# Top-k attention and two MLPs on one core: the planner's DMA prices are changed and the order of the work is searched again

## The chip, the cores and the metric

The kernel runs on one core of a Trainium2 chip. The metric is the device time of one execution in microseconds, the median over several runs. TensorE does matrix products, VectorE and ScalarE element work and reductions, GpSimd element work, and SyncE issues all DMA transfers of this kernel, plain and transposing ones.

## What is computed

The inputs are q, k and v of 4 batches, 8 heads, 576 positions and 64 dimensions. Each row of scores keeps its 32 largest entries, and a softmax over these weighs v. The heads are joined to 2304 tokens of 512 values, and two MLPs of 512 to 2048 to 512 follow, the first with a softplus and the second with h - tanh(h) as its nonlinearity:

```python
scores = scale * np.matmul(q, k.transpose(0, 1, 3, 2))
kth = np.partition(scores, -top_k, axis=-1)[..., -top_k:-top_k + 1]
scores = np.where(scores >= kth, scores, -1000000000.0)
attn = softmax(scores)                 # top_k = 32
x = np.matmul(attn, v)                 # heads joined: 2304 x 512
x = softplus(x @ w_in) @ w_out
h = x @ w_in2
out = (h - np.tanh(h)) @ w_out2
```

## The kernel before, in words

All matrix products are done in pairs of 16-bit numbers: each operand is split into a high and a low half, and three products replace one.

**Attention.** A visit is a pair of heads of one batch and two of its four blocks of 128 queries (32 visits). `visit_load` (L1198) loads q, k and v; `visit_prep_k` and `visit_prep_q` (L1233, L1269) scale and split k and q and transpose them by DMA into kT and qT. Where k and v serve a second visit, they are parked in device memory (kd, vd) and fetched back. A visit has four tiles of 128 x 576 scores, and half of the visits have one tile more for the left-over 64 queries of each head. For each tile, `front` (L1320) makes scores on TensorE, which ScalarE copies out; `chain` (L1368) runs seven selections on VectorE (four times the 8 largest, three times replacing them); `exps` (L1383) and `turn` (L1408) form the masked exponentials, split them into hl and issue the DMA transpose into pT; `back` (L1421) multiplies pT with v on TensorE and, after the second head, transposes the result into a chunk's input.

**Weights.** The four weight matrices come in eight groups each through `weight_load`, `weight_convert` and `weight_split` (L855 to L955), with work on ScalarE, VectorE, GpSimd and TensorE for each group. `norm` (L1010) reads the tensors a second time for a scale of each batch.

**MLPs.** Chunks of 256 tokens (and two of 128 left-over tokens) go through `mlp_step` (L1624), one group of weights a step: `gemm1`, the nonlinearity (`act1`), `gemm2`. The first MLP of a chunk needs its attention tiles, the second needs the first one's scale.

**The order.** Nothing is issued while the program text above runs. A `Recorder` (L230) keeps each engine call as an operation with a price from `price` (L319). `order` (L548) starts from the order of the text with random noise on each rank (seed `SEED`, spread `SIG`), plans forwards and backwards seven times in `place` (L440), keeps the best plan, and adds the noise of every entry of `SHIFTS`: a random seed or the names of steps, a stretch of planned time in ns, a spread or an offset in ns, and the letters of the engines (P, D, A, G, S for TensorE, VectorE, ScalarE, GpSimd, SyncE). The plan that results is the order in which each engine's queue is written out by `run` (L647, the calls themselves at L658, which is why all rows of the trace name L658). `idle` (L585) puts small keep-busy matmuls into planned gaps of TensorE.

In the plan a DMA takes SyncE's time (the first number that `price` gives), and then its traffic (the second) on one queue that all transfers share; it has landed `DLAT` later:

```python
busy = max(busy, t + 800) + o.lat
end[i] = busy + DLAT            # DLAT = 1700
```

SyncE's queue is strictly in order, so an issue that waits for its source holds all issues behind it.

Of the kernel before, what the change touches and what calls it, by code (L numbers as in the profile page):

```python
# [78 lines left out]
SEED = 219  # L79
# [5 lines left out]
SIG = 15  # L85
# [35 lines left out]
MARGP = 0.0  # L121

SHIFTS = (
# [15 lines left out]
    ("S", 201532, 209532, -1000, "PDAGS"), (30793, 419293, 427293, 1000, "PDAGS"), (3088, 194840, 202840, 400, "PDAGS"),  # L139
# [7 lines left out]
    (11067, 946337, 986337, 1000, "PDAGS"), (44392, 990466, 1030466, 6000, "PDAGS"), (82429, 1039495, 1047495, 2500, "PD"),  # L147
    (2374, 229658, 237658, 1000, "PDAGS"), (99569, 810939, 830939, 400, "SA"), (72260, 653623, 673623, 1000, "PDAGS"),
# [15 lines left out]
    (30152, 681321, 689321, 1000, "PDAGS"), (37243, 797248, 817248, 200, "PDAGS"), (88929, 199096, 219096, 200, "SA"),  # L164
# [6 lines left out]
    (3405, 588701, 738701, 200, "PDAGS"), (89568, 201552, 209552, 400, "PDAGS"), (4446, 719529, 759529, 100, "PD"),  # L171
# [58 lines left out]
class Recorder:  # L230
# [88 lines left out]
    def price(self, eng, method, a, k, outs, ins):  # L319
        out = outs[0]  # L320
# [10 lines left out]
        if eng == "SP":  # L331
            size = math.prod(out.shape) * mybir.dt.size(out.dtype)
            if "transpose" in method:
                return 1350.0, size / 164.0
# [1615 lines left out]
```

## Time and profile before

| | before |
|---|---|
| median of 3 runs | 1143.07 us (1141.26 to 1143.63) |
| the profiled execution | 1143.22 us |
| its span, first to last instruction | 1141.5 us |
| TensorE busy, matmuls | 90% of the span |
| VectorE, ScalarE, GpSimd busy | 82%, 80%, 66% |
| DMA issues on SyncE | 411 plain, 304 transposing |

The rows below come from that profiled execution, and times in them count from the span's start. PE is TensorE (PEld its weight loads), DVE is VectorE, ACT is ScalarE, POOL is GpSimd, and SPq is SyncE's queue of issues. Tile names are those of the program with the numbers left out: s are the scores, h and y the accumulators of the MLPs, px the attention output, hl the split exponentials.

### The profile page before, as it was taken

Reading aid. Unit: us, or ns where it says so; the run is one execution under the profiler, and the core shown is the slowest. Engines: PE = TensorE matmul, PEld = TensorE weight load, DVE = VectorE, ACT = ScalarE, POOL = GpSimd, SP = SyncE. Lnnn points to the kernel's source line nnn. Section 1 sums busy time; section 2 is a strip of 40 time slices with the busy share of each in tenths; the row PEclk is TensorE's granted clock in tenths of the full one; section 3 lists DMA queues with packets and bytes.
Section 4 is the critical chain, followed back from the end, with each engine's and each line's share of the span. In section 5 each row is a group of like instructions: output and inputs, shape, how many; then the busy total and the mean of one; then the engine's idle time right before and its main releaser. Section 6 shows DMA issues by size and latency. Waiting matters only on the chain.

```text
span 1141.5 us, 27974 instructions
## 1 busy us (share of the span) xinstructions
PE 1027.5 (90%) x10094; PEld 795.4 (70%) x10094; DVE 931.3 (82%) x2059; ACT 913.1 (80%) x1889; POOL 757.2 (66%) x1169
## 2 busy tenths in 40 slices
PE   4577647988989899999989999999999999999998
PEld 2334336866658777876689868976787789977965
DVE  3888989989999999999989999999999999510111
ACT  6999999999888998888889888898978777732422
POOL 3445445999778777667878677788976677543433
PEclk9698767999999999999999999999999999999999
DMA  8999997557769875546877655466665443200000
GB/s 270 286 242 253 263 237 214 166 115 157 139 150 199 168 143 102 117 86 124 185 170 150 127 107 113 78 126 131 162 119 106 78 108 70 49 6 19 2 8 22
DMA packets 323131, 153.15 MB, mean 134 GB/s; under 512 B 270256, under 2 KB 314288, under 8 KB 322992
## 3 DMA queue, kind: packets, MB, share of 16 engines
q1 hardware_dynamic: 322992, 151.36, 59.4%
q8 instruction: 79, 1.29, 0.5%
q14 instruction: 60, 0.49, 0.1%
HBM read 73.01 MB, written 15.37 MB: 77 GB/s over the span
## 4 chain that ended last, share of the span: by engine, by line
PE 49%; ACT 18%; DVE 11%; POOL 7%; DMA 7%; issue 6%; SPq 2%; ACTq 0%; POOLq 0%; DVEq 0%
PE y L658 21%; PE h L658 20%; DVE x L658 5%; PE s L658 4%; DVE m L658 4%; ACT x L658 3%; ACT ssb L658 3%; PE px L658 3%; ACT wlo L658 2%; ACT xy L658 2%; SPq L658 2%; POOL hl L658 2%; ACT hl L658 2%; ACT r L658 1%; ACT whi L658 1%
## 5 line engine op out<-in xcount | busy, mean ns | idle before, releaser
L658 PEld LDWEIGHTS <-whi 128*128 128x128 f16 (+1 forms) x3994 | 372.7, 99 | 101.4 <-DVE whi L658 27.1
L658 PE MATMUL h<-xy,whi 128*128 128x256 f16 (+1 forms) x2560 | 395.0, 262 | 5.1 <-ACT r L658 4.1
L658 PE MATMUL h<-xy,wlo 128*128 128x256 f16 (+1 forms) x1280 | 324.9, 262 | 0.0
L658 DVE MAX8 m<-x 128x8 f32<-128x576 f32 x432 | 314.9, 747 | 1.0
L658 POOL TENSOR_TENSOR hl<-x,hl 128x512 f16<-128x512 f32 (+1 forms) x288 | 213.1, 757 | 80.0 <-ACT hl L658 71.3
L658 PEld LDWEIGHTS <-wlo 128*128 128x128 f16 (+1 forms) x2002 | 197.1, 99 | 33.5 <-issue 13.9
L658 DVE MATCH_REPLACE8 x<-m,x 128x576 f32<-128x576 f32 x288 | 212.9, 740 | 0.0
L658 PE MATMUL y<-g,whi 128*128 128x256 f16 (+1 forms) x1280 | 199.4, 262 | 1.1 <-POOL g L658 1.1
L658 PE MATMUL y<-whi,g 128*128 128x512 f16 x576 | 194.2, 380 | 0.6 <-POOL g L658 0.6
L658 POOL TENSOR_TENSOR g<-r,g 128x512 f16<-128x512 f32 (+1 forms) x160 | 173.5, 1085 | 14.8 <-PE y L658 8.4
L658 PE MATMUL y<-g,wlo 128*128 128x256 f16 (+1 forms) x640 | 162.5, 262 | 0.0
L658 DVE SCALAR_TENSOR_TENSOR r<-h,hinb,r 128x512 f32<-128x512 f32 (+1 forms) x80 | 55.0, 687 | 122.4 <-ACT r L658 122.1
L658 PEld LDWEIGHTS <-g 128*128 128x128 f16 x864 | 81.6, 98 | 74.7 <-POOL g L658 1.3
L658 ACT ACTIVATE x<-ssb,nb,tiny 128x576 f32<-128x576 f32 x136 | 117.5, 865 | 6.7 <-POOL nb L658 4.2
L658 DVE MAX8 m<-ssb 128x8 f32<-128x576 f32 x144 | 107.6, 747 | 16.1 <-ACT ssb L658 12.5
L658 PEld LDWEIGHTS <-pT 128*128 128x128 f16 (+1 forms) x2240 | 87.8, 102 | 35.0 <-DMA pT<-hl 15.9
L658 PE MATMUL y<-wlo,g 128*128 128x512 f16 x288 | 109.4, 380 | 0.0
L658 DVE MATCH_REPLACE8 x<-m,ssb 128x576 f32<-128x576 f32 x144 | 106.6, 740 | 0.0
L658 PE MATMUL px<-vhl,pT 128*128 128x65 f16 (+1 forms) x2240 | 95.3, 196 | 11.8 <-DMA pT<-hl 9.4
L658 PE MATMUL s<-kT,qT 128*128 128x288 f16 x512 | 87.4, 295 | 16.6 <-ACT ssb L658 7.8
L658 POOL TENSOR_SCALAR r<-r,gsb 128x512 f32<-128x512 f32 (+1 forms) x80 | 53.8, 673 | 67.9 <-ACT g L658 65.0
L658 ACT CAST hl<-x 128x576 f16<-128x576 f32 x144 | 96.6, 671 | 2.1 <-DMA pT<-hl 2.0
(134 smaller groups left out, 1665.2 us busy)
## 6 DMA issues: line engine op xcount, KB each, us to landing
whi<-in_moe_w_in_dram SPq DMA_DIRECT2D x11, 1023.0 KB, 6.9
whi<-in_moe_w_out_dram SPq DMA_DIRECT2D x7, 1023.5 KB, 6.0
vd<-vhl SPq DMA_DIRECT2D x16, 330.0 KB, 3.5
vhl<-vd SPq DMA_DIRECT2D x16, 330.0 KB, 3.8
kd<-kT SPq DMA_DIRECT2D x32, 160.0 KB, 2.8
kT<-kd SPq DMA_DIRECT2D x32, 160.0 KB, 3.0
xy<-in_moe_w_out_dram SPq DMA_DIRECT2D x18, 255.8 KB, 3.1
qraw<-in_q_dram SPq DMA_DIRECT2D x64, 64.0 KB, 2.5
```

The lines of the kernel that those rows point to most:

```text
L658: fn(*a, **k)
```

## The change

In `price`, a DMA issue on SyncE and the traffic of a transposing DMA are priced anew, by size; the constants `PTC` and `SPC` are new; `SEED` and `SIG` have other values, and `SHIFTS` has other entries throughout. The operations that are recorded are the same. The condition on 128,000 elements takes in pT (128 x 9 x 128) and qT (128 x 8 x 128); the other transposes (kT, the chunk input, the left-over queries) are below it. The list of `SHIFTS` is cut to an entry of each.

```diff
-SEED = 219
+SEED = 12130
...
-SIG = 15
+SIG = 150
...
+PTC = 1600.0
+SPC = 640.0
 
 SHIFTS = (
-    (65854, 156749, 196749, 100, "PD"), (28308, 218614, 226614, 200, "PDAGS"), (28963, 611250, 761250, 1000, "S"),
...
+    (46389, 1013650, 1033650, 6000, "P"), ("L3", 21785, 321785, -1000, "PDAGS"), (76838, 41833, 101833, 2500, "S"), (75144, 482483, 502483, 400, "A"),
...
         if eng == "SP":
             size = math.prod(out.shape) * mybir.dt.size(out.dtype)
             if "transpose" in method:
-                return 1350.0, size / 164.0
-            return 540.0, size / 330.0
+                return (PTC if math.prod(out.shape) >= 128 * 1000 else 1335.0), size / 230.0
+            kb = size // 1024
+            return (770.0 if kb == 32 else 690.0 if kb == 16 else 550.0 if kb in (230, 232) else SPC), size / 330.0
```

## Rows read from the trace of the kernel before

**Rows 1.** The head of the page: busy us, share of the span, instructions.

```profile
span 1141.5 us, 27974 instructions
PE 1027.5 (90%) x10094; PEld 795.4 (70%) x10094; DVE 931.3 (82%) x2059; ACT 913.1 (80%) x1889; POOL 757.2 (66%) x1169
```

**Rows 2.** Stretches: length, busy us of PE, PEld, DVE, ACT, POOL, clock, DMA share, GB/s.

```profile
0.00:100.00 100.00, 61.66 (x331) 34.27 (x332) 69.59 (x171) 84.65 (x169) 42.71 (x74) 0.86 0.96 271
100.00:200.00 100.00, 63.19 (x502) 43.41 (x501) 95.96 (x209) 94.71 (x192) 51.04 (x75) 0.73 0.95 234
...
250.00:300.00 50.00, 42.95 (x423) 33.07 (x422) 46.81 (x117) 44.55 (x107) 44.70 (x77) 0.97 0.67 137
300.00:350.00 50.00, 43.71 (x441) 31.65 (x439) 47.18 (x103) 45.13 (x96) 40.78 (x67) 1.00 0.70 154
350.00:400.00 50.00, 45.53 (x488) 39.37 (x485) 47.46 (x99) 45.04 (x100) 38.04 (x58) 1.00 0.86 180
...
550.00:600.00 50.00, 44.98 (x490) 39.84 (x491) 46.76 (x94) 43.01 (x90) 38.85 (x59) 1.00 0.84 177
...
1000.00:1142.00 142.00, 137.41 (x1160) 101.97 (x1158) 16.80 (x33) 47.89 (x78) 52.58 (x68) 1.00 0.04 11
```

**Rows 3.** Waits of PE, 300 to 400 us: total us, times, longest.

```profile
PE px L658 <- DMA pT<-hl: 4.6, 3, 2.5
...
PE s L658 <- DMA kT<-khl: 1.7, 1, 1.7
...
PE px L658 <- DMA ql<-in_q_dram: 0.3, 1, 0.3
```

**Rows 4.** Waits of PE, 500 to 600 us.

```profile
PE s L658 <- DMA kT<-khl: 2.2, 1, 2.2
...
PE px L658 <- DMA pT<-hl: 0.3, 1, 0.3
```

**Rows 5.** Chain of waits, 300 to 400 us: shares by line, two pieces (start, us).

```profile
by line: ACT x L658 11.2%; issue 11.2%; SPq L658 10.7%; ACT ssb L658 8.2%; ACT r L658 6.8%; PE h L658 4.3%; ACT hl L658 4.2%; DMA xy<-in_q_dram 4.0%; ACT g L658 3.7%; ACT xy L658 3.6%; DMA pT<-hl 3.2%; DMA out_dram<-r 2.9%; ACT vhl L658 2.5
...
318.10 2.77 SPq L658
320.92 2.07 DMA kraw<-in_k_dram
```

**Rows 6.** SyncE's issues in order of time: start us, us; 99 before the last.

```profile
301.40 1.23 SPq L658 DMA_TRANSPOSE qT<-qhl  x1
...
400.26 1.27 SPq L658 DMA_TRANSPOSE qT<-qhl  x1
```

**Rows 7.** DMA issues, 300 to 400 us: the transposes, count, us to landing.

```profile
pT<-hl SPq DMA_TRANSPOSE x16, 3.5
...
xy<-xs SPq DMA_TRANSPOSE x10, 3.0
kT<-khl SPq DMA_TRANSPOSE x8, 3.2
...
qT<-qhl SPq DMA_TRANSPOSE x5, 3.1
...
qlT<-zq SPq DMA_TRANSPOSE x1, 3.6
```

**Rows 8.** The tile hl on SyncE, 0 to 200 us: issue ns min/median/max, landing.

```profile
L658 SPq DMA_TRANSPOSE pT<-hl x19: 1247/1672/3048, 38.2 to 185.5; - x19
...
DMA to landing us min/median/max: 3.2/4.9/8.0
```

**Rows 9.** The same tile, 200 to 1000 us.

```profile
L658 SPq DMA_TRANSPOSE pT<-hl x125: 1241/1302/2449, 202.0 to 994.9; - x125
...
DMA to landing us min/median/max: 3.2/3.4/5.8
```

More of the change, by code (lines that the diff above doesn't have):

```diff
@@ L121 @@
 MARGP = 0.0
+PTC = 1600.0
+SPC = 640.0
 SHIFTS = (
[15 rows of a table removed]
-    ("S", 201532, 209532, -1000, "PDAGS"), (30793, 419293, 427293, 1000, "PDAGS"), (3088, 194840, 202840, 400, "PDAGS"),
[7 rows of a table removed]
-    (11067, 946337, 986337, 1000, "PDAGS"), (44392, 990466, 1030466, 6000, "PDAGS"), (82429, 1039495, 1047495, 2500, "PD"),
-    (2374, 229658, 237658, 1000, "PDAGS"), (99569, 810939, 830939, 400, "SA"), (72260, 653623, 673623, 1000, "PDAGS"),
[15 rows of a table removed]
-    (30152, 681321, 689321, 1000, "PDAGS"), (37243, 797248, 817248, 200, "PDAGS"), (88929, 199096, 219096, 200, "SA"),
[6 rows of a table removed]
@@ L171 @@
-    (3405, 588701, 738701, 200, "PDAGS"), (89568, 201552, 209552, 400, "PDAGS"), (4446, 719529, 759529, 100, "PD"),
[3 rows of a table removed]
-    (17909, 633166, 693166, 400, "PDAGS"), (74182, 365812, 373812, 2500, "PDAGS"), (56364, 400295, 420295, 400, "PDAGS"),
-    (50012, 680208, 688208, 100, "PDAGS"), (68348, 383507, 443507, 100, "PDAGS"), (76410, 778623, 786623, 400, "SA"),
-    (75530, 760685, 800685, 100, "PDAGS"), (50157, 374022, 382022, 6000, "P"), (53770, 707888, 715888, 2500, "S"),
[5 rows of a table added]
+    (19788, 400133, 420133, 400, "PDAGS"), ("S", 163120, 183120, -1000, "PDAGS"), (33840, 34058, 42058, 400, "PDAGS"),
@@ new lines @@
+    (91963, 167971, 317971, 200, "PDAGS"), (12879, 782422, 932422, 200, "SA"), (27238, 666144, 686144, 400, "PDAGS"),
[6 rows of a table added]
+    (2845, 4981, 12981, 200, "PDAGS"), ("M0", 235551, 243551, 20000, "PDAGS"), ("N3", 88964, 2000000, 1000, "PDAG"),
[14 rows of a table added]
+    (25487, 951743, 959743, 6000, "PDAGS"), ("W2", 119002, 127002, -20000, "PDAGS"), (72190, 952161, 992161, 6000, "PDAGS"),
+    (92249, 94967, 154967, 400, "A"), (85508, 225447, 245447, 400, "A"), ("", 84359, 104359, 6000, "PDAGS"), (89908, 58046, 78046, 1000, "P"),
@@ new lines @@
+    (31139, 640882, 660882, 2500, "PD"), (92698, 518700, 526700, 6000, "S"), (79721, 490224, 510224, 1000, "P"),
+    ("P,V", 145208, 153208, -3000, "PDAGS"), (24195, 952178, 972178, 6000, "PDAGS"), (5990, 993454, 1033454, 6000, "PDAGS"),
[8 rows of a table added]
+    ("N1", -1000000, 2000000, 1000, "PDAG"), (39132, 752468, 760468, 6000, "SA"), ("P,V", 18550, 26550, 20000, "PDAG"),
[5 rows of a table added]
+    (21444, 206084, 356084, 400, "S"), ("P,V", 207673, 227673, 1000, "PDAG"), (42558, 1058825, 1098825, 6000, "PDAGS"),
[7 rows of a table added]
+    (6879, 321015, 329015, 1000, "PDAGS"), (94692, 660386, 668386, 1000, "PDAGS"), (90813, 273459, 281459, 1000, "PDAGS"),
[3 rows of a table added]
@@ new lines @@
+    (76968, 457854, 477854, 200, "PDAGS"), (16248, 233733, 241733, 400, "SA"), (79456, 536193, 576193, 100, "PDAGS"),
[4 rows of a table added]
+    (16761, 658114, 678114, 1000, "PDAGS"), ("P,V", 288782, 296782, 1000, "PDAGS"), (77901, 263268, 283268, 100, "PDAGS"),
+    (66200, 283996, 291996, 2500, "G"), (78609, 444485, 452485, 2500, "PDAGS"), (23524, 311989, 461989, 200, "P"), (76392, 617559, 637559, 2500, "G"),
+    (2987, 588914, 608914, 200, "PDAGS"), (11702, 219958, 239958, 200, "PDAGS"), (37011, 586508, 606508, 6000, "P"),
@@ L178 @@
+    (51336, 618911, 678911, 200, "PDAGS"), (44460, 645705, 653705, 200, "PDAGS"), (50763, 654609, 662609, 400, "SA"),
[4 rows of a table added]
 )
```

100 rows, old and new, of the table SHIFTS are left out of this document.

## The prediction

> **What bounds the kernel now.** I read the head of the page first: which engine is busiest. TensorE leads with 1027.5 us of a span of 1141.5 us, and VectorE and ScalarE follow within ten points [rows 1]. No instruction is meant to change its work, so what a new order can move is the part of the span in which TensorE stands idle: 1141.5 - 1027.5 = 114.0 us. The table of stretches says where it lies [rows 2]. The first 100 us hold 100 - 61.66 = 38.3 us of it and the second 36.8 us; 250 to 300 us holds 7.1, 300 to 400 us holds 6.29 + 4.47 = 10.8, 550 to 600 us holds 5.0. The last 142 us are TensorE's alone (137.41 us busy, VectorE 16.80), so the end is set by TensorE, and every microsecond that it stops idling earlier ends the program a microsecond sooner, as long as the work that it would do is ready.
>
> The two idle parts have different causes. From 0 to 200 us the clock is also low: the granted clock is 0.86 and then 0.73, so TensorE ran partly at 1.2 and partly at 2.4 GHz; the DMA engines are 0.96 and 0.95 busy, and in the second 100 us VectorE and ScalarE are at 95.96 and 94.71 us [rows 2]. That opening is full on four resources at once. From 300 to 400 us nothing but VectorE is as full, yet TensorE waits. There I asked for TensorE's waits: 4.6 us for the transposed probabilities (pT), 1.7 us for transposed keys, 0.3 us behind a query load, 6.6 us together, all of them for DMAs [rows 3]. In 500 to 600 us it is 2.2 + 0.3 = 2.5 us [rows 4].
>
> The chain of waits through 300 to 400 us shows SyncE's queue with 10.7% of that stretch, beside DMA landings of 4.0, 3.2 and 2.9%; one piece of it is an issue of 2.77 us on SyncE, directly followed by the landing of a key load that had queued behind it [rows 5]. SyncE's own sequence of issues says why: the first issue after 301.40 us and the one at 400.26 us are 98.86 us apart, with 99 issues back to back [rows 6]. The list of DMA issues has the 99 by kind; 16 + 5 + 10 + 8 + 1 = 40 are transposes [rows 7], so 59 are plain. SyncE's queue is the pace there.
>
> **The change, part by part.** It alters prices in the planner and the random draws by which it orders the work, and so the order on all five engines' queues. Transfers, tiles and arithmetic stay: by instruction the sum of removed and added work is nothing. Only the small keep-busy matmuls that the planner puts into planned TensorE gaps can change in number; they stand in gaps, and I cost them at nothing. If a gap is smaller on the chip than planned, they lie on TensorE's path, and the plan's gaps differ between both kernels by no amount that a row shows.
>
> *Issue prices.* Old prices of the 99 issues: 40 x 1.35 + 59 x 0.54 = 85.9 us, against 98.86 us in the trace. New prices: pT and the transposed queries have over 128,000 elements, so 21 x 1.6 us, the other 19 x 1.335 us, and the 59 plain ones at the default of 0.64 us (some sizes have 0.55 to 0.77): 33.6 + 25.4 + 37.8 = 96.7 us. So in this stretch the old planner thought SyncE some 13 us faster than it is, the new one 2 us. What it put on TensorE for the moment in which a transpose should have landed came late on the chip; a planner that knows this puts other matmuls there or issues the transpose ahead of loads that can wait. What it can win is the wait for DMAs on TensorE, 6.6 us [rows 3] and 2.5 us [rows 4]: I take both whole, **-9.1 us**. The bounds: nothing at the upper end, because another late input can take each wait's place (ScalarE sits at 45 of 50 us in both halves of 300 to 400 us); at the lower end all of TensorE's idle time in the two stretches, 10.8 + 5.0 = 15.8 us. I take the waits since they are the row nearest to what the edit touches.
>
> *Overpriced issues.* After 200 us a pT issue takes 1.302 us in the middle of 125 [rows 9], so 1.6 us is too much there by 0.3 us less the gap between two issues; in the opening it takes 1.672 us [rows 8], and 1.6 is right. The planner will leave SyncE about a quarter of a microsecond of room per pT. I cost it at 0: TensorE has matmuls of the two MLPs queued, which need no pT. Without that cover, TensorE would be given a pT later than it could have it; the bounds are 0 and a loss of 2.5 us, the waits of the weaker stretch [rows 4], since a plan that waits needlessly can at worst undo what it won there.
>
> *Traffic prices.* A pT moves 128 x 9 x 128 x 2 = 294,912 bytes: 1.80 us of queue before at 164 bytes per ns, 1.28 us after at 230. With the 0.8 us to start and 1.7 us to land that the planner adds, an unhindered pT lands after 4.3 us by the old price and 3.8 us by the new; the trace has 3.4 us after 200 us [rows 9], so the new price is the better one for 125 of 144. In the opening it has 4.9 us [rows 8], and there the old price is nearer. The 19 pT of the opening are now 19 x 0.52 = 9.8 us cheaper in the plan, in a stretch whose DMA engines the trace shows full. I take 0 for the opening, since VectorE, ScalarE and the DMAs are all full there and an order cannot shorten them; bounds are 9.8 us to either side, the one amount by which the plan of the opening is known to move.
>
> Queues passed: since every order is drawn anew, an issue on SyncE that is moved ahead holds all behind it for 1.3 us (transpose) or about 0.6 us (plain), whoever waits for them; the 2.77 us piece above is the worst that the chain shows [rows 5].
>
> The sum: the profiled execution took 1143.22 us for its span of 1141.5, 0.15 us above the median of 1143.07. 1143.22 - 9.1 = 1134.1, on the scale of the median **1134.0 us**.
>
> A rule against this: the Trainium skill, page "DMA: Bandwidth & Descriptors", section "Issuing engines are not separate DMA queues", says that the sequencer's time to start a DMA is usually small relative to the DMA itself. By that rule issue prices would decide nothing and the sum would be 0, at 1143.1 us. This case's trace does not agree for 300 to 400 us, where 99 issues fill 98.86 us.
>
> **The rivals.** *No change, 1143.1 us.* The waits for DMAs are real but not binding: when TensorE gets pT earlier, it meets the next late thing, ScalarE's copies or VectorE's selection, which run at 47 of 50 us in 300 to 400 us. For it: VectorE is nearly full there. Against it: TensorE's own waits name DMAs for 6.6 of its 10.8 us of idle time there [rows 3]. The same result would come if the change did not do what it says because plain orders barely move; the much wider first draw (150 in place of 15) speaks against that. Chance 0.17.
>
> *Slower, 1152.9 us.* The one mechanism: the opening. The plan now has 9.8 us less DMA time for the same pT transfers, packs weight and norm loads into it, and on the chip the engines are already 0.96 busy [rows 2], so the weights' last groups and the first transposes land later by that much. It decides when that lateness is more than VectorE's and ScalarE's queued work covers; taken whole, 1143.1 + 9.8 = 1152.9 us. For it: 4.9 us to land in the opening against 3.8 planned. Against it: TensorE has so much idle time there that lateness may be absorbed. Chance 0.23.
>
> *Much faster, 1117.5 us.* The new draw also finds a better opening: 1143.1 - 15.8 - 9.8. For it: 75.1 us idle on TensorE by 200 us and 30.4 us on VectorE in the first 100. Against it: no price that governs the opening's arithmetic was touched. Chance 0.10.
>
> **How the numbers follow.** My own case, TensorE's waits for DMAs shrinking, has 0.50 and its own range is 1127 (1143.1 - 15.8) to 1141. With 0.2% (2.3 us, about what a measurement of this kernel can tell from no change), faster is 0.50 + 0.10 = 0.60, same 0.17, slower 0.23. The range that should hold 8 in 10 reaches down to 1121, leaving out the better part of the much faster case, and up to 1152, just short of the slower rival's whole price: 1121 to 1152 us, predicted 1134.0.
>
> **What would show it.** Right: TensorE's busy time stays near 1027 us and its idle time falls; waits of TensorE for pT and transposed keys in the stretch where SyncE issues back to back fall from 6.6 us to under 3; 99 issues still take about 99 us. Slower rival: idle time of TensorE up to 200 us grows beyond 75 us, with pT landing above 4.9 us there. No change: the waits for DMAs are gone, but waits for ScalarE or VectorE of the same size stand in their place. The forecast is wrong if the idle time moves mainly in stretches where neither SyncE nor the DMA engines are full: then the draws, not the prices, made the difference.

## The result, and the profile after

The changed kernel takes 1127.92 us, the median of 4 runs, against 1143.34 us for the kernel before (with a fourth run); the ratio is 0.9871, with a 95% interval from 0.9854 to 0.9888. The profiled execution took 1127.21 us, with a span of 1125.5 us. Forecast were 1134.0 us and a range from 1121 to 1152 us.

The head of the changed kernel's page, with the first line of its chain of waits:

```profile
span 1125.5 us, 27898 instructions
PE 1022.8 (91%) x10078; PEld 796.4 (71%) x10078; DVE 921.3 (82%) x2059; ACT 913.8 (81%) x1889; POOL 751.7 (67%) x1169
...
PE 51%; ACT 16%; DVE 13%; POOL 8%; issue 6%; DMA 5%; SPq 0%; POOLq 0%; ACTq 0%; DVEq 0%
```

Against [rows 1], TensorE is idle for 1125.5 - 1022.8 = 102.7 us in place of 114.0 us, and busy for 4.7 us less; together that is the 16.0 us between the two spans. VectorE, ScalarE and GpSimd have the same number of instructions. SyncE's queue has gone from the chain; in the kernel before it had 2% of it:

```profile
PE 49%; ACT 18%; DVE 11%; POOL 7%; DMA 7%; issue 6%; SPq 2%; ACTq 0%; POOLq 0%; DVEq 0%
```

The changed kernel by stretches, with the columns of [rows 2]:

```profile
0.00:100.00 100.00, 56.62 (x310) 31.75 (x311) 67.28 (x165) 83.23 (x165) 39.86 (x77) 0.85 1.00 281
100.00:200.00 100.00, 66.41 (x497) 45.60 (x497) 95.28 (x214) 94.39 (x197) 48.53 (x74) 0.74 0.90 229
...
250.00:300.00 50.00, 40.92 (x435) 32.59 (x434) 49.85 (x121) 45.50 (x108) 44.95 (x79) 0.97 0.66 142
300.00:350.00 50.00, 49.90 (x474) 37.37 (x471) 49.18 (x115) 47.00 (x101) 44.57 (x70) 1.00 0.75 156
350.00:400.00 50.00, 46.47 (x485) 39.51 (x484) 47.40 (x104) 46.19 (x100) 40.06 (x60) 0.97 0.81 178
...
550.00:600.00 50.00, 50.00 (x602) 45.56 (x600) 49.80 (x105) 46.36 (x98) 45.92 (x67) 1.00 0.84 172
...
1000.00:1126.00 126.00, 121.18 (x1003) 89.64 (x1000) 13.93 (x25) 42.48 (x68) 47.12 (x60) 1.00 0.03 12
```

The opening has not gained: up to 200 us TensorE is busy for 56.62 + 66.41 = 123.0 us, before 124.85, at much the same granted clock (0.85 and 0.74). From 300 to 400 us its idle time falls from 10.8 to 0.10 + 3.53 = 3.6 us, and in 550 to 600 us from 5.0 to none.

TensorE's waits in the changed kernel, first all of 300 to 400 us and then all of 500 to 600 us:

```profile
PE s L678 <- ACT ssb L678: 3.2, 2, 1.7
PE s L678 <- DVE n L678: 0.3, 1, 0.3
...
PE s L678 <- ACT ssb L678: 0.2, 1, 0.2
```

No wait for a DMA is left in either stretch; [rows 3] had 6.6 us and [rows 4] 2.5 us of them. SyncE is about as full as it was:

```profile
300.92 1.23 SPq L678 DMA_TRANSPOSE qT<-qhl  x1
...
399.83 0.57 SPq L678 DMA_DIRECT2D kraw<-in_k_dram  x1
```

These are the first and the last issue of the same stretch in the changed kernel, in the form of [rows 6]; 97 issues start between 300 and 400 us, where the kernel before had 99. What changed is mainly which issue stands where, not how many there are.

**The plan and the chip.** `order` gives each of SyncE's 715 issues a planned start. They keep their sequence on the chip, so planned and measured starts can be subtracted one by one; this is the mean lag of the chip behind the plan in us:

```
issues that start in   150-200  250-300  350-400  450-500  600-650  900-950
kernel before             10.3     18.4     27.6     28.7     37.2     39.9
changed kernel            12.2     17.6     21.2     21.4     21.6     24.2
```

Both orders fall behind alike up to 300 us. Then the old one loses 9.2 us between 250-300 and 350-400 us and 8.5 us between 450-500 and 600-650 us; the new one loses 3.6 and 0.2 us there. In the kernel before, these two steps enclose the stretches in which SyncE hardly pauses: from 300 to 400 us there are three pauses of more than 0.2 us between two issues, 2.2 us together, and from 542 to 596 us there is none. The old plan promised transposes earlier than SyncE could start them.

### The profile page after: what moved, and what is told of

Its sections match the earlier page's. It is cut to its first block, busy times and chain, and to the rows that moved or that the text cites. A ratio compares the mean times of both kernels' runs of the same rounds, so it can differ in the third digit from the quotient of the medians.

```text
span 1125.5 us, 27898 instructions
## 1 busy us (share of the span) xinstructions
PE 1022.8 (91%) x10078; PEld 796.4 (71%) x10078; DVE 921.3 (82%) x2059; ACT 913.8 (81%) x1889; POOL 751.7 (67%) x1169
## 4 chain that ended last, share of the span: by engine, by line
PE 51%; ACT 16%; DVE 13%; POOL 8%; issue 6%; DMA 5%; SPq 0%; POOLq 0%; ACTq 0%; DVEq 0%
PE h L678 23%; PE y L678 21%; DVE x L678 5%; DVE m L678 5%; PE s L678 5%; PE px L678 3%; ACT ssb L678 3%; ACT x L678 3%; POOL hl L678 2%; ACT wlo L678 2%; ACT whi L678 2%; ACT hl L678 2%; ACT r L678 1%; POOL g L678 1%; DMA pT<-hl 1%
## 5 line engine op out<-in xcount | busy, mean ns | idle before, releaser
L678 PE MATMUL y<-g,whi 128*128 128x256 f16 (+1 forms) x1280 | 197.1, 262 | 0.2 <-DVE xy L678 0.2
L678 PE MATMUL s<-kT,qT 128*128 128x288 f16 x512 | 86.0, 292 | 18.6 <-ACT ssb L678 11.1
L678 ACT COPY ssb<-s 128x576 f32<-128x576 f32 x144 | 91.4, 635 | 9.3 <-PE s L678 8.5
```

The source lines that it names most:

```text
L678: fn(*a, **k)
```

## The experiments

Two explanations have to be told apart: that the right prices made the gain, and that any new search would have found it. For a fair comparison the prices were varied and the order was searched again under each set, always until the kernel's own plan ended at the same point (about 1100 us on its own prices), with other random draws than the changed kernel's and with `SIG = 15.0`, the spread of before. If the prices do not matter, all of these take the same time.

### Which prices: both, none, or one kind

Each experiment keeps the changed kernel's program. `s1_old_old` and `s2_old_old` (two sets of draws) undo both kinds of prices:

```diff
-                return (PTC if math.prod(out.shape) >= 128 * 1000 else 1335.0), size / 230.0
-            kb = size // 1024
-            return (770.0 if kb == 32 else 690.0 if kb == 16 else 550.0 if kb in (230, 232) else SPC), size / 330.0
+                return 1350.0, size / 164.0
+            return 540.0, size / 330.0
...
 SEED, SIG and SHIFTS: found by a search of its own
```

`s1_new_new` undoes neither and has other draws only. `s1_issue_only` undoes the traffic price (`size / 230.0` becomes `size / 164.0`), `s1_traffic_only` undoes the issue prices (the first three lines above, with `1350.0, size / 230.0`).

Expected of `s1_old_old`:

> Old issue prices and old traffic prices, order searched anew with other random draws until its own plan ended at 1100 us, the same end that the three kernels beside it were searched to. Theory 1 (the corrected issue prices made the gain): about where before is, 1138 to 1146 us, with TensorE idle again for 8 to 12 us between 300 and 400 us. Rival (a fresh draw made the gain, prices did not matter): 1124 to 1132 us, as the changed kernel.

Of `s1_new_new`:

> New issue prices and new traffic prices, other random draws than the changed kernel's, searched until its plan ended at 1100 us. Theory 1: 1124 to 1132 us, TensorE idle under 5 us between 300 and 400 us. Rival: the same, since it is a fresh draw too.

Of `s1_issue_only`:

> New issue prices with the old traffic price for transposes, searched until its plan ended at 1100 us. Theory 1: near the changed kernel, 1125 to 1133 us. Second rival (the traffic price made the gain): 1138 to 1146 us.

Of `s1_traffic_only`:

> Old issue prices with the new traffic price for transposes, searched until its plan ended at 1100 us. Theory 1: near before, 1137 to 1147 us. Second rival (the traffic price made the gain): 1125 to 1133 us.

Of `s2_old_old`:

> Old issue prices and old traffic price once more, with a second set of random draws, searched until its plan ended at 1100 us. Theory 1: 1140 to 1152 us, as before and as the first set of draws. If the first set was merely unlucky: 1124 to 1136 us.

Measured:

| | issue prices | traffic price | median us | ratio to before | 95% interval |
|---|---|---|---|---|---|
| changed kernel | new | new | 1127.92 | 0.9871 | 0.9854 to 0.9888 |
| s1_new_new | new | new | 1126.04 | 0.9841 | 0.9810 to 0.9873 |
| s1_issue_only | new | old | 1124.78 | 0.9831 | 0.9799 to 0.9864 |
| s1_traffic_only | old | new | 1152.92 | 1.0083 | 1.0052 to 1.0114 |
| s1_old_old | old | old | 1147.92 | 1.0027 | 1.0005 to 1.0050 |
| s2_old_old | old | old | 1136.78 | 0.9937 | 0.9914 to 0.9959 |

All orders found with the new issue prices lie below all orders found with the old ones, and the traffic price makes no gain in either company. The draws matter too: with identical old prices two sets of draws are 11.1 us apart. `s2_old_old` came out between its two branches, `s1_traffic_only` 5.9 us above its range, `s1_old_old` 1.9 us above, `s1_issue_only` 0.2 us below.

Where the difference arises is best seen in how many matmuls TensorE gets through while SyncE paces the kernel, from 300 to 700 us. First the kernel before and the changed kernel (columns as in [rows 2]; the count behind TensorE's busy time is what to compare):

```profile
300.00:700.00 400.00, 379.25 (x3991) 300.66 (x3989) 385.62 (x841) 349.68 (x740) 299.90 (x465) 1.00 0.67 139
```

```profile
300.00:700.00 400.00, 394.03 (x4139) 315.90 (x4137) 392.14 (x882) 361.67 (x766) 311.32 (x481) 1.00 0.71 144
```

That is 148 matmuls more and 20.8 - 6.0 = 14.8 us less idle time. Over the whole span idle time falls by 11.3 us, since 3.3 us of this are lost again before 300 us. The same stretch of `s1_new_new`, `s1_issue_only`, `s1_traffic_only`, `s1_old_old` and `s2_old_old`, in this order:

```profile
300.00:700.00 400.00, 390.32 (x4136) 313.21 (x4134) 391.92 (x872) 358.68 (x760) 312.25 (x477) 1.00 0.68 144
```

```profile
300.00:700.00 400.00, 391.83 (x4140) 313.64 (x4139) 391.41 (x875) 360.49 (x763) 312.17 (x481) 1.00 0.72 143
```

```profile
300.00:700.00 400.00, 379.92 (x3919) 299.29 (x3918) 375.46 (x829) 345.36 (x731) 297.66 (x459) 0.98 0.69 138
```

```profile
300.00:700.00 400.00, 381.18 (x3972) 301.19 (x3971) 379.81 (x842) 351.43 (x744) 302.34 (x467) 1.00 0.69 140
```

```profile
300.00:700.00 400.00, 382.16 (x4015) 304.99 (x4012) 384.45 (x847) 352.05 (x742) 301.78 (x464) 1.00 0.68 140
```

With the new issue prices 4136 to 4140, with the old ones 3919 to 4015; of the two later kernels with the new issue prices, one has 4142 and one 4065. `s2_old_old` owes part of its better time to another place. The stretch up to 300 us, first of the kernel before and then of `s2_old_old`:

```profile
0.00:300.00 300.00, 213.76 (x1695) 150.34 (x1696) 254.82 (x595) 270.69 (x573) 186.65 (x299) 0.86 0.85 216
```

```profile
0.00:300.00 300.00, 216.05 (x1739) 152.53 (x1740) 264.63 (x602) 275.66 (x585) 190.58 (x308) 0.87 0.84 218
```

It has 44 matmuls more behind it by then. That reads as luck of the draw: up to 300 us the changed kernel has 1706, `s1_old_old` 1639, `s1_new_new` 1715, `s1_issue_only` 1700 and `s1_traffic_only` 1688, which do not sort by prices.

An equal end of the plan is not an equal search, since with dearer issues an order has to be better to end at 1100 us. The kernels themselves answer this: each one's order can be held fixed and its start times worked out again, by the planner's own rules, with other prices. With the old issue prices and the new traffic price, the seven orders compared here all end between 1097.9 and 1103.5 us, so by the old prices the new orders are not better searched. With all new prices the orders found with the old issue prices would end at 1115.5 to 1128.2 us, the others at 1098.1 to 1099.8 us, and the chip took 21 to 30 us longer than that for each of the seven. The old prices do not see the difference that the chip shows, and the new ones do.

TensorE's waits for DMAs from 300 to 400 us in `s1_old_old`:

```profile
PE px L659 <- DMA pT<-hl: 4.5, 4, 1.4
PE s L659 <- DMA kT<-khl: 1.8, 3, 1.5
```

The waits of [rows 3] are back, with 6.3 us, in an order that shares no draw with the kernel before. `s2_old_old` has 5.7 us of waits for DMAs there, `s1_traffic_only` 4.9, `s1_issue_only` none. But `s1_new_new` has some too, 3.3 us:

```profile
PE px L659 <- DMA pT<-hl: 2.2, 2, 1.6
PE s L659 <- DMA kT<-khl: 1.1, 2, 0.6
```

So these waits are smaller under the new issue prices and not always gone. `s1_new_new` also has more idle time there than the 5 us expected of it, 3.07 + 3.58 = 6.7 us (TensorE is busy for 46.93 and 46.42 us of the two halves).

### Plain issues and transposes apart

`s1_plain_price` has the new prices for plain issues and `1350.0` for all transposes, `s1_transpose_price` the new prices for transposes and `540.0` for all plain issues; both keep the new traffic price.

```diff
-                return (PTC if math.prod(out.shape) >= 128 * 1000 else 1335.0), size / 230.0
+                return 1350.0, size / 230.0
...
-            return (770.0 if kb == 32 else 690.0 if kb == 16 else 550.0 if kb in (230, 232) else SPC), size / 330.0
+            return 540.0, size / 330.0
```

The first pair of lines is `s1_plain_price`, the second `s1_transpose_price`.

> New prices for plain issues alone (transposes 1.35 us as before, traffic price new), searched until its plan ended at 1100 us. Over the 99 issues of the stretch read before, plain prices give 40 x 1.35 + 59 x 0.64 = 91.8 us of the 98.9: somewhat more than half of the missing time. Theory 1 in proportion: 1129 to 1139 us. If the price of the large transposes is what counts: 1143 to 1155 us.

> New prices for transposing issues alone (plain issues 0.54 us as before, traffic price new), searched until its plan ended at 1100 us. Over the 99 issues: 21 x 1.6 + 19 x 1.335 + 59 x 0.54 = 90.8 us of 98.9, so somewhat less than half of the missing time is restored. Theory 1 in proportion: 1130 to 1141 us. If plain issues are what counts: 1143 to 1155 us.

Measured: 1136.34 us for plain prices alone (ratio 0.9928, 0.9900 to 0.9956) and 1136.89 us for transposing prices alone (0.9922, 0.9899 to 0.9946). Their stretch from 300 to 700 us:

```profile
300.00:700.00 400.00, 385.56 (x4031) 305.59 (x4029) 386.55 (x859) 357.32 (x754) 306.06 (x471) 1.00 0.69 143
```

```profile
300.00:700.00 400.00, 384.33 (x3985) 303.14 (x3984) 381.88 (x850) 351.20 (x747) 301.30 (x467) 0.99 0.68 141
```

Neither price alone brings TensorE to some 4140 matmuls. Both times lie between the two ends, as expected of prices that are half right, but `s2_old_old` took 1136.78 us with neither price corrected. So it is not shown that one of the two prices alone gains anything, nor which counts for more.

### One half of the change without the other

`prices_only` has all new prices with the `SEED`, `SIG` and `SHIFTS` of before; `draws_only` has the old prices with those of the changed kernel.

```diff
 prices_only
-SEED = 12130
+SEED = 219
...
-SIG = 150
+SIG = 15
...
 draws_only
-                return (PTC if math.prod(out.shape) >= 128 * 1000 else 1335.0), size / 230.0
+                return 1350.0, size / 164.0
```

> All new prices, with the seed, the spread and the list of shifts of before: the prices without the new search. The shifts were found for another plan, so the plan that comes out is not a searched one. Theory 1 with search needed for both halves: slower than before, 1146 to 1158 us. If right prices by themselves help: 1125 to 1140 us.

> Old prices with the changed kernel's seed, spread and list of shifts: the draws without the prices. Theory 1: much slower than before, 1158 to 1178 us, an unsearched plan made with wrong prices. Rival (the new draws carry the gain): 1125 to 1135 us.

Measured: 1145.45 us for the prices alone (ratio 1.0003, 0.9986 to 1.0021), 1164.98 us for the draws alone (1.0170, 1.0135 to 1.0205). The first lies just below its slower branch, the second inside its own. The list of shifts is tied to the plan that it was found for: the two plans end at 1122.7 and 1127.3 us instead of about 1100. With right prices the chip takes only some 23 us more than the plan says, so that the kernel is as fast as before, whose plan ends at 1099.6 us and which takes some 44 us more; with wrong prices the changed kernel's own list loses 1.7%. So the gain is in neither half by itself: it needs a search, and a search under right issue prices.

### Is the price of the large transposes too high?

`s1_pt_1420` has `PTC = 1420.0` in place of `1600.0` and was searched to the same end of its plan.

```diff
-PTC = 1600.0
+PTC = 1420.0
```

> New prices, but the issue of the large transposes at 1.42 us, near the trace's 1.3 us after 200 us and the gap to the next issue, in place of 1.6 us; searched until its plan ended at 1100 us. If 1.6 us is too much after 200 us and the room it leaves on SyncE costs time: 1118 to 1124 us. If the room costs nothing, as the prediction has it: 1124 to 1130 us. If what 1.6 us adds (slack for issues that are held up) is what helps: 1130 to 1137 us.

Measured: 1135.29 us (ratio 0.9925, 0.9906 to 0.9944), 4017 matmuls from 300 to 700 us:

```profile
300.00:700.00 400.00, 383.85 (x4017) 304.11 (x4018) 389.97 (x855) 353.19 (x749) 303.25 (x465) 1.00 0.70 142
```

The lower price gives the slower kernel, by 7 to 9 us against the changed kernel and `s1_new_new`. This is the third branch, a price that leaves slack for issues that are held up. It is one set of draws; since two sets with equal prices have differed by 11.1 us, it is a sign and not a proof. The order itself speaks for the price: held fixed and timed with all new prices, it would end at 1109.4 us, where the changed kernel's ends at 1098.1, and the chip again took 26 us more.

The kernel before shows why 1.42 us need not be the more faithful price. Where SyncE is full, what an issue costs the queue is the time until the next issue can start, with the held-up ones counted. Two pT and the issues behind them, the first held up:

```profile
303.57 2.15 SPq L658 DMA_TRANSPOSE pT<-hl  x1
305.77 0.57 SPq L658 DMA_DIRECT2D qraw<-in_q_dram  x1
...
314.20 1.29 SPq L658 DMA_TRANSPOSE pT<-hl  x1
315.55 0.57 SPq L658 DMA_DIRECT2D kraw<-in_k_dram  x1
```

From the start of a pT to the next issue it is 1.64 us on average for the 16 pT of 300 to 400 us (1.55 without one pause of 1.5 us), and 1.62 us for the nine of 542 to 596 us. For the 59 plain issues of 300 to 400 us it is 0.63 us, of which the issue itself is 0.54. The new prices of 1.6 and 0.64 us lie at these means; the old 0.54 us left out the step to the next issue. For the five transposed queries, which have the same price as pT, the mean is 1.32 us, so for them 1.6 us is too much.

### Other wrong prices

`pool_new` and `pool_old_traffic` also correct two prices of GpSimd, under the new issue prices, and were searched for longer.

```diff
-            return 35 + 1.9 * n if out.dtype == F32 else 50.0 + n, 100.0
+            return 35 + 1.9 * n if out.dtype == F32 else (240.0 if n >= 256 else 50.0) + n, 100.0
...
-            return 335.0 + MRX if n == 1 else 245.0 if n <= 8 else 225 + 0.85 * n, 100.0
+            return 335.0 + MRX if n == 1 else 245.0 if n <= 8 else 340 + 0.85 * n, 100.0
```

> New prices, and two prices of GpSimd corrected as well: its wide multiplications by a column 0.115 us dearer, its wide 16-bit fills 0.19 us dearer; searched for longer, to a plan that ends at 1101 us. If wrong prices on other engines still cost time: 1115 to 1123 us. If SyncE's were the ones that mattered: 1124 to 1130 us.

> New issue prices, the old traffic price for transposes, and the two GpSimd prices corrected; searched for longer, to a plan that ends at 1100 us. If the GpSimd prices matter: 1113 to 1122 us, the fastest of all. If not: 1122 to 1128 us, as the kernel with the new issue prices alone.

Measured: 1132.51 us (ratio 0.9910, 0.9885 to 0.9936) and 1128.52 us (0.9864, 0.9845 to 0.9883). The first is slower than either branch had it, the second just above the upper one. Their stretch from 300 to 700 us:

```profile
300.00:700.00 400.00, 386.27 (x4065) 308.93 (x4064) 393.51 (x866) 355.50 (x753) 303.78 (x475) 1.00 0.69 143
```

```profile
300.00:700.00 400.00, 392.31 (x4142) 314.51 (x4140) 393.40 (x875) 359.26 (x761) 310.14 (x479) 1.00 0.71 144
```

Nothing was won by these two prices and the longer search. `pool_new` also bounds the main result: with the new issue prices a draw can give as little as 4065 matmuls, and its interval overlaps that of `s2_old_old`. Over the kernels with all issue prices new or all old, each searched under its own prices, the five with the new ones take 1124.8 to 1132.5 us, and the four with the old, the kernel before included, 1136.8 to 1152.9 us. The groups do not overlap, and between single members the difference is anything from 4 to 28 us.

The fastest kernel of the study is `s1_issue_only`, 1.7% below before. Its interval overlaps that of the changed kernel (0.9799 to 0.9864 against 0.9854 to 0.9888), so it beats before, and is not shown to beat the change.

## Why the prediction was right, point by point

**The bound.** TensorE's idle time was taken as what an order can move, and SyncE's queue as the pace from 300 to 400 us. Both held: the kernels differ mainly by what TensorE gets done from 300 to 700 us, and that goes with the issue prices.

**The issue prices, -9.1 us.** The sign and the place were right, the term was too small. It counted the waits that the profile puts down to DMAs, 6.6 us from 300 to 400 and 2.5 us from 500 to 600 us, and these went to nothing. But the idle time fell further, from 10.8 to 3.6 us in the first stretch and from 6.7 to 0.3 us in the second:

```profile
500.00:600.00 100.00, 93.31 (x931) 72.51 (x929) 96.19 (x205) 86.06 (x179) 78.29 (x121) 1.00 0.68 144
```

```profile
500.00:600.00 100.00, 99.72 (x1055) 79.90 (x1053) 99.60 (x220) 92.22 (x190) 88.49 (x138) 1.00 0.76 148
```

That is 13.5 us, with 1.2 us more between 400 and 500 and between 600 and 700 us. The prediction called TensorE's waits "all of them for DMAs". That holds for the three rows that it added up; the kernel before had others in the same stretches, first from 300 to 400 and then from 500 to 600 us:

```profile
PE s L658 <- ACT ssb L658: 2.5, 2, 1.8
PE y L658 <- POOL g L658: 0.9, 2, 0.6
PE h L658 <- ACT r L658: 0.5, 1, 0.5
```

```profile
PE h L658 <- ACT r L658: 3.6, 3, 1.8
PE h L658 <- DVE r L658: 0.5, 1, 0.5
```

Of these the ones for r and g went as well, 5.5 us, and only the one for ScalarE's copies (ssb) stayed, 2.5 us before and 3.4 after. That late transposes had held up these engines too, so that their lateness was SyncE's once more, would explain it; no run shows it. Taking the waits because they were "the row nearest to what the edit touches" was the step that failed in size; of the lower end, 15.8 us of idle time from 300 to 400 and 550 to 600 us, some 12 us came. The size is also in part the draw's, as the spread of the searched kernels says.

**The rule against it.** The Trainium skill, page "DMA: Bandwidth & Descriptors", section "Issuing engines are not separate DMA queues", calls a sequencer's time to start a DMA usually small relative to the DMA itself. This case does not agree: a pT takes 1.302 us to issue and 3.4 us to land [rows 9], and with equal plan ends the new issue prices are worth 1152.92 - 1126.04 = 26.9 us with the new traffic price and 12.0 or 23.1 us with the old one, draws included.

**Overpriced issues, 0.** The room left on SyncE did not show as a cost: the kernel with the lower price was not faster but slower, by one set of draws. The reading behind the term was wrong: it took the middle pT issue, 1.302 us, and left out the held-up ones, with which a pT takes SyncE 1.55 to 1.64 us where its queue is full. There 1.6 us leaves little room.

**The traffic price, 0 in the opening.** Right within the noise of the draws: `s1_issue_only` does as well without the new traffic price as `s1_new_new` with it. The slower rival's mechanism shows faintly in the changed kernel. The tile hl on SyncE, 0 to 200 us, as in [rows 8]:

```profile
L678 SPq DMA_TRANSPOSE pT<-hl x19: 1272/1602/4863, 42.0 to 194.0; - x19
...
  PEld L678: 11.3, 4
...
DMA to landing us min/median/max: 3.2/5.0/6.9
```

In the kernel before, the row of the weight loads was:

```profile
  PEld L658: 4.2, 4
```

The weight loads of TensorE wait 11.3 us for pT there in place of 4.2, pT takes 5.0 us to land in place of 4.9, and TensorE's idle time up to 200 us has grown from 75.1 to 77.0 us: 1.8 us of the 9.8 that the rival could have cost. Both signs of the slower rival came, if barely, and its price did not. Why it was not more was not tried by itself.

**TensorE's busy time** was said to stay near 1027 us; it fell by 4.7 us, which the prediction has no term for. The keep-busy matmuls are not the reason: the page's total falls by 16 of 10094, and at about 0.1 us each they are worth under 2 us. The rest is not explained by a run.

**The sum.** Between the two spans lie 16.0 us: 14.8 us less idle time from 300 to 700 us, 3.3 us more before 300 us, 0.2 us more after 700 us, and 4.7 us less busy time. The opening of the changed kernel up to 300 us, to be held against that of the kernel before above:

```profile
0.00:300.00 300.00, 210.42 (x1706) 150.23 (x1706) 256.68 (x597) 271.38 (x575) 182.54 (x300) 0.86 0.83 217
```

The measured 1127.92 us is 6.1 us below the forecast of 1134.0: the issue prices brought more than forecast, the busy time fell without a term for it, and the opening took some of this back.

**What would have made it wrong** did not come: of the 14.8 us of idle time, 13.5 us went from 300 to 400 and from 500 to 600 us, which hold the stretches in which SyncE hardly pauses.

## What to carry to other kernels

Where a planner orders the work, compare its planned start with the trace's start of the same instruction, stretch by stretch: the lag grew here where a price was wrong, and that stretch, not the share of the engine in the whole span, says what correcting the price is worth. Price an operation of a queue that runs in order by the mean time until the next one can start, with the held-up ones counted, and not by the middle one's own time. After a price is corrected the search must be made again; shifts found for one set of prices can cost time under another. Size such a gain with all idle time of the bounding engine in the stretch in view, not by the waits alone that name the mispriced resource, and test it against more than one set of random draws, since these alone moved this kernel by 11 us.

## What the runs showed of the hardware that was not expected

Starting the same transpose does not always take SyncE the same time. In the opening the median issue of pT took 1.602 us in the changed kernel, and one took 4.863 us; after 200 us the median is 1.305 us (before 1.672 and 1.302 us [rows 8, 9]):

```profile
L678 SPq DMA_TRANSPOSE pT<-hl x125: 1241/1305/2295, 206.3 to 987.4; - x125
```

The DMA engines are fuller in the opening, with a DMA share of 0.90 to 1.00, but that is not shown to be the cause. The transposes of the chunk inputs (xs) take as long there as later; in the kernel before, up to 200 us and from 200 to 1000 us:

```profile
L658 SPq DMA_TRANSPOSE xy<-xs x8: 1167/1204/1272, 79.9 to 178.0; - x8
```

```profile
L658 SPq DMA_TRANSPOSE xy<-xs x71: 1158/1195/2788, 260.8 to 998.9; - x71
```

What holds an issue of pT in the opening stays open. One price for it cannot be right in all stretches.
